# Two kinds of stores issued from Pool's queue, and a new plan of PSUM copies and of the turn to the last stage, in an attention and two feed-forward layers

## The chip, the cores and the metric

One core of a Trainium2 chip runs the whole program. The metric is the device time of one execution in microseconds. Engines are named as in the profile: PE is TensorE's matmul, PEld its weight load, DVE is VectorE, ACT ScalarE, POOL GpSimd, SP SyncE.

## What is computed

A windowed causal attention, then a feed-forward layer with two multiplied branches and two further products, then a second one with a squared ReLU. Everything is fp32.

```python
# attention: B, H, S, D = 4, 8, 576, 64; window 128
scores = np.matmul(q, k.transpose(0, 1, 3, 2)) / np.sqrt(D)
rel = pos[:, None] - pos[None, :]
mask = (rel >= 0) & (rel < window)
scores = np.where(mask, scores - slopes[:, None, None] * np.abs(rel), -1e9)
attn = softmax(scores)            # over the last axis
x = (attn @ v).transpose(0, 2, 1, 3).reshape(B * S, H * D)      # 2304 x 512
# first layer: w1, w2 512 x 1024; w3 1024 x 1024; w_out 1024 x 512
x = (((x @ w1) * (x @ w2)) @ w3) @ w_out
# second layer: w_in 512 x 2048; w_out 2048 x 512
h = np.maximum(x @ w_in, 0.0)
out = (h * h) @ w_out
```

## The kernel before, in words

**Arithmetic.** Outside the attention every fp32 product is made from two fp32r parts of each operand, a high and a low one, in three matmuls (the lines 929 to 931 in the first layer, 1125 to 1127 after it). ScalarE makes the high part by a copy (L196), VectorE or Pool the low one by a subtraction (L199). Blocks of 2 x 2 are multiplied with seven products instead of eight, P1 to P7, so VectorE and Pool also form sums of operands (L716) and of results (L950, L978, L981, L1189, L1236), and ScalarE copies results out of PSUM (tiles d, D, E).

**Stages.** (1) The attention takes 16 pairs of heads. Per pair PE makes the scores (L437) in a first and a second part, VectorE adds the bias and takes the minimum (L405), ScalarE takes the exponent (L413), VectorE the reciprocal of the sums (L422, L423), and `scaled` (L248) normalises on VectorE (L252), ScalarE (L254) or Pool (L250). PE transposes the result (L473), which is copied from PSUM to the tile pt (L196 on ScalarE, L258 on VectorE), multiplies it with v (L497, L513; `p_pv`, `p_pvl`), and `t_xh` copies that product back into the same pt buffer, from which `t_xs` (L526) stores it to x_scr in DRAM. pt has two buffers. While that runs, PE makes the product of w3 with w_out as work of low rank (`p_w34`, L613), which is copied to sg and stored to w_scr by `t_w34` (L621). (2) x is loaded again, split, and multiplied with w1 and w2 (sums d, stored to g_scr). (3) The result times the product of w3 and w_out gives y. (4) y times w_in, with ReLU, goes to s_scr (tiles D). (5) The last stage loads blocks of s_scr (A11, A12, A21, A22; L1297), squares them (L1305), forms sums (L1319), splits them (tiles xA, ww) and multiplies by the second w_out, whose words were merged earlier (`m_scr`) and are loaded back by `m_back`, combined and split (`add_words2`) for each of eight row blocks; "wlao7" is the low part of the last block's word, "wlbo7" that of its sums.

**Order.** Nothing is ordered by hand row by row. The class `Plan` (L31 to L147) is a list scheduler that runs on the host when the program is built: each task has a rank, its engines with a cost, its predecessors, and the buffers it takes and gives back. It keeps a clock per engine; for each task that is ready it picks the engine with the earliest end, to which `bias` (L44) adds a penalty per engine ("d" VectorE, "D" VectorE with a lock shared with "p", Pool; "a" ScalarE), and among the tasks that can start first the one with the lowest rank (`RANK`, L16). If PE would stand still for over 1 us ahead of 40 us of the plan it inserts three small matmuls of an identity, fillers (`p_warm`, L528). The instructions are then written in the plan's order, so each engine and each DMA queue has a fixed order; a latency table (L293) tells the plan how long a result takes to the next engine. "gate" tasks open and close pools: `q1`, `ph`, `q2` (L651 to L669 and L1426 to L1430); q2, the pool of the last stage, takes the place of q1. The list `turn` (L1456) gives the order of the products where the last stage begins. P1 and P2 of the first block are cut in two: Q1 and Q2 accumulate over the row blocks 0 to 5 of the words (18 matmuls each), P1 and P2 over the last two (6 matmuls each); P4 and the others are whole.

All stores and loads are issued by SyncE, one queue, in the plan's order. The tasks of the two stores at issue:

```python
add(f"sx{m}", r + 9, {"dma": w_dma(295)}, lambda e: t_xs(m), [f"xh{g}_{m}" for g in range(2)], [], [f"pt_{m}"])
add(f"sw{fi}", -10, {"dma": w_dma(262)}, lambda e: t_w34(fi), [f"wh{fi}"], [], [f"sg{fi}"])
```

## Time and profile before

| what | value |
|---|---|
| median of 3 runs | 808.65 us (806.52 to 810.44) |
| the profiled execution | 812.59 us, of which the span is 810.8 |
| TensorE busy | 791.7 us of the span |
| VectorE, ScalarE, Pool busy | 612.7, 510.7, 67.9 us |
| mean granted clock of TensorE | 0.989 |
| bytes moved | 155.80 MB, 192 GB/s over the span |

The profile shows one execution. Its span goes from the first to the last instruction; the time of the execution is 1.8 us longer. Busy time counts an engine's instructions; an instruction that issues a DMA is not counted. "A <- B: 2.1, 3, 0.8" in a table of waits means that A's engine stood idle 2.1 us in all, 3 times, 0.8 us at the longest, until B had ended. In a timeline the bracket behind a row gives the idle time ahead of it and what ended it. A granted clock of 1.00 is the full rate.

### The profile page before, as it was taken

What the parts mean: (1) busy time and instruction counts of PE and PEld (TensorE: products, weight loads), DVE (VectorE), ACT (ScalarE), POOL (GpSimd) and SP (SyncE); (2) the same over time, 40 slices, a digit from 0 to 9 for tenths busy, and PEclk for the clock granted to TensorE, in tenths of its full rate; (3) what the DMA queues carried; (4) which work ended last, traced back from release to release, by engine and by line L of the source; (5) the groups of instructions that cost most, each with busy time, mean ns of one, the idle gap of its engine ahead of it and who ended that gap; (6) DMA issues with size and microseconds to landing.
All of it is one profiled execution on the core that took longest, in us unless ns stands there. A gap on an engine that the chain in (4) does not pass through costs nothing. (4 is left out here: it accounts for less than half of the span.)

```text
span 810.8 us, 17310 instructions
## 1 busy us (share of the span) xinstructions
PE 791.7 (98%) x6582; PEld 735.0 (91%) x6582; DVE 612.7 (76%) x1291; ACT 510.7 (63%) x1090; POOL 67.9 (8%) x65
## 2 busy tenths in 40 slices
PE   7989999999999999999999999999998999999998
PEld 6755666689999999899999999999998999999998
DVE  6778687989887787978899955325768997777762
ACT  6988789974554545545655756646766776656630
POOL 1000020111010000200102300001213100000000
PEclk8989999999999999999999999999999999999999
DMA  9987899525887888366754453525654765544200
GB/s 221 289 272 262 250 307 272 179 94 173 308 277 267 279 288 282 123 203 216 219 195 162 160 195 103 201 99 197 203 186 136 193 178 156 142 130 131 79 27 33
DMA packets 115699, 155.80 MB, mean 192 GB/s; under 512 B 12192, under 2 KB 92576, under 8 KB 113568
## 3 DMA queue, kind: packets, MB, share of 16 engines
q1 hardware_dynamic: 115616, 154.70, 61.0%
q8 instruction: 51, 0.84, 0.5%
q14 instruction: 32, 0.26, 0.1%
HBM read 101.71 MB, written 52.95 MB: 191 GB/s over the span
## 5 line engine op out<-in xcount | busy, mean ns | idle before, releaser
L196 ACT ACTIVATE d<-xa 128x288 f32<-128x288 f32 x128 | 52.2, 409 | 97.4 <-PE xa L931 93.3
L1189 DVE TENSOR_TENSOR D<-xb,D 128x384 f32<-128x384 f32 (+1 forms) x62 | 32.1, 520 | 59.3 <-ACT D L196 34.9
L413 ACT ACTIVATE e<-e,st 128x128 f32<-128x128 f32 (+1 forms) x144 | 62.2, 435 | 6.4 <-DVE st L405 5.4
L613 PE MATMUL g<-raw 128*128 128x512 f32 x128 | 63.0, 602 | 0.4 <-DVE raw L335 0.4
L199 DVE TENSOR_TENSOR ww<-fq,ww 128x1024 fp32r<-128x1024 f32 x34 | 41.6, 1223 | 27.0 <-ACT ww L196 26.8
L196 ACT ACTIVATE D<-xa 128x384 f32<-128x384 f32 (+1 forms) x91 | 41.8, 462 | 30.0 <-PE xa L1127 26.4
L196 ACT ACTIVATE ww<-fq 128x1024 fp32r<-128x1024 f32 x35 | 36.9, 1057 | 36.8 <-PE xa L1127 19.9
L931 PE MATMUL xa<-xB,u 128*128 128x288 f32 x192 | 56.8, 296 | 0.0
L929 PE MATMUL xa<-xB,u 128*128 128x288 f32 x192 | 56.8, 296 | 0.0
L930 PE MATMUL xa<-xB,u 128*128 128x288 f32 x192 | 56.1, 292 | 0.0
L1262 ACT ACTIVATE D<-D 128x384 f32<-128x384 f32 x73 | 37.4, 521 | 23.3 <-DVE D L1189 23.3
L716 DVE TENSOR_TENSOR xA<-xA 128x256 f32<-128x256 f32 (+2 forms) x74 | 47.7, 669 | 3.0 <-DMA xA<-g_scr 1.5
L950 DVE TENSOR_TENSOR d<-xb,d 128x288 f32<-128x288 f32 x80 | 36.2, 452 | 15.2 <-ACT d L196 10.8
L473 PEld LDWEIGHTS t<-ident,e 128*128 128x128 f32 x208 | 24.4, 144 | 23.6 <-ACT pt L196 11.2
L405 DVE CUSTOM_DVE_ANT_0 e<-s,bw 128x192 f32<-128x192 f32 (+1 forms) x128 | 40.4, 351 | 2.9 <-PE s L437 2.6
L437 PE MATMUL s<-qk 64*64 64x128 f32 (+2 forms) x768 | 37.5, 293 | 5.0 <-issue 2.1
L437 PEld LDWEIGHTS s<-qk 64*64 64x64 f32 x768 | 28.9, 140 | 13.0 <-issue 4.8
L473 PE MATMUL t<-ident,e 128*128 128x128 f32 x208 | 36.8, 291 | 1.7 <-ACT pt L196 1.3
L930 PEld LDWEIGHTS xa<-xB,u 128*128 128x128 f32 x192 | 36.5, 190 | 0.0
L929 PEld LDWEIGHTS xa<-xB,u 128*128 128x128 f32 x192 | 36.1, 188 | 0.0
L931 PEld LDWEIGHTS xa<-xB,u 128*128 128x128 f32 x192 | 36.0, 188 | 0.0
L1127 PE MATMUL xa<-yA,v 128*128 128x384 f32 x104 | 35.2, 339 | 0.0
(272 smaller groups left out, 2897.9 us busy)
## 6 DMA issues: line engine op xcount, KB each, us to landing
s_scr<-D SPq DMA_DIRECT2D x96, 192.0 KB, 2.0
u<-in_w2io_dram SPq DMA_DIRECT2D x32, 512.0 KB, 6.0
xA<-s_scr SPq DMA_DIRECT2D x20, 512.0 KB, 5.4
qk<-in_qk_dram SPq DMA_DIRECT2D x32, 288.0 KB, 5.4
g_scr<-d SPq DMA_DIRECT2D x64, 144.0 KB, 3.3
xA<-g_scr SPq DMA_DIRECT2D x16, 576.0 KB, 5.5
raw<-in_w3t_dram SPq DMA_DIRECT2D x8, 1024.0 KB, 9.0
raw<-in_w_dram SPq DMA_DIRECT2D x8, 1024.0 KB, 6.9
```

Of the source, the lines that this page charges most:

```text
L196: nc.scalar.activation(out=o, in_=i, func=ACTF.Copy)
L199: eng.tensor_tensor(out=o, in0=a, in1=b, op=ALU.subtract)
L405: nc.vector.tensor_tensor_reduce(out=part_of(m, x, rows), in0=ps, in1=bias, op0=ALU.add, op1=ALU.min, scale=-0.125, scalar=3.0e38, accum_o ...
L413: nc.scalar.activation(out=e, in_=e, func=ACTF.Exp, bias=st[:, 0, x:x + 1], scale=-1.0, accum_out=st[:, 1, x:x + 1],)
L437: nc.tensor.matmul(HD[2 * m + r]["s"][g][o, c:c + w], t[h, 0, 64 * q:64 * q + 64], t[h, 1, 64 * k:64 * k + w], start=True, stop=True,)
L473: nc.tensor.transpose(o, e[:, u:u + 2, :].rearrange("p u c -> p (u c)"), ident)
L613: nc.tensor.matmul(gw[fi], wl, wr, start=c == 0, stop=c == 7)
L716: ENG[e].tensor_tensor(out=o(oi), in0=a(ai), in1=b(bi), op=op)
L929: nc.tensor.matmul(o, wh, xh, start=start and c == 0, stop=False, skip_group_check=True)
L930: nc.tensor.matmul(o, wh, xl, start=False, stop=False, skip_group_check=True)
L931: nc.tensor.matmul(o, wl, xh, start=False, stop=c == len(todo) - 1, skip_group_check=True)
L1262: nc.scalar.activation(out=x, in_=x, func=ACTF.Relu)
```

## The change

It has seven parts. (a) The 16 x stores and the 8 stores of the product are issued from Pool's queue; the plan gets a key "q" for it, with a cost of 1.0 on Pool and a latency of 3.5. (b) The plan's penalties on VectorE fall: d from 1.0 to 0.6, D from 0.2 to 0. (c) The attention's rank h0 goes from -40 to -44. (d) The sums of the last word of the second w_out get a tile of their own, xQ, in the pool q1, in place of xA. (e) The first block's load of A21 waits for the last word, and the split of A12 for its P2 goes to a tile xA in place of u. (f) The gate q2 waits for wlbo7 too. (g) In the list `turn` Q2 stands ahead of P1.

```diff
-RANK = dict(..., c0=0, cj=3, h0=-40, hs=7, ...)
+RANK = dict(..., c0=0, cj=3, h0=-44, hs=7, ...)
...
-    bias = dict(d=1.0, D=0.2, a=0.3, p=0.0)
+    bias = dict(d=0.6, D=0.0, a=0.3, p=0.0)
...
-                    e = q.lower()
+                    e = "p" if q == "q" else q.lower()
...
-            end[n], on[n] = fin, e
+            end[n], on[n] = fin, q if q == "q" else e
...
-                last[h] = max(last[h], fin + (self.lat[e] + 0.5 if e == "dma" else 0.0))
+                last[h] = max(last[h], fin + (self.lat[on[n]] + 0.5 if on[n] in ("dma", "q") else 0.0))
...
-            yA=14, t2a=1, v6=6, D1=2, D2=2, D4=2, D3=1, E1=2, fq=5, ww=4,
+            yA=14, t2a=1, xQ=1, v6=6, D1=2, D2=2, D4=2, D3=1, E1=2, fq=5, ww=4,
...
-        dict(pe=0.25, a=0.3, d=0.22, p=0.25, dma=3.0, gate=0.0),
+        dict(pe=0.25, a=0.3, d=0.22, p=0.25, dma=3.0, gate=0.0, q=3.5),
...
     def t_xs(m):
         b, p = divmod(m, H // 2)
-        nc.sync.dma_start(out=x_scr[b][p], in_=PR[m]["pt"][:, 0:S])
+        nc.gpsimd.dma_start(out=x_scr[b][p], in_=PR[m]["pt"][:, 0:S])
...
-        add(f"sx{m}", r + 9, {"dma": w_dma(295)}, lambda e: t_xs(m), [f"xh{g}_{m}" for g in range(2)], [], [f"pt_{m}"])
+        add(f"sx{m}", r + 9, {"q": 1.0}, lambda e: t_xs(m), [f"xh{g}_{m}" for g in range(2)], [], [f"pt_{m}"])
...
     def t_w34(fi):
-        nc.sync.dma_start(out=w_scr[fi], in_=gw.pop(fi))
+        nc.gpsimd.dma_start(out=w_scr[fi], in_=gw.pop(fi))
...
-        add(f"sw{fi}", -10, {"dma": w_dma(262)}, lambda e: t_w34(fi), [f"wh{fi}"], [], [f"sg{fi}"])
+        add(f"sw{fi}", -10, {"q": 1.0}, lambda e: t_w34(fi), [f"wh{fi}"], [], [f"sg{fi}"])
...
-        pool.update(yA=q, t2a=q, D1=q)
+        pool.update(yA=q, t2a=q, D1=q, xQ=q)
...
-            mw[k, m], sw[k, m] = new(tag, [128, 1024]), new(tag, [128, 768])
+            mw[k, m], sw[k, m] = new(tag, [128, 1024]), new("xQ" if (k, m) == ("o", NM - 1) else tag, [128, 768])
...
-            hold(ss, stag, 6)
+            hold(ss, "xQ" if (k, m) == ("o", NM - 1) else stag, 6)
...
-                + ([] if t == 0 else [f"lf{k}{t - 1}", "wlbo7", ...] if k in ("A11", "A21") else [f"fc1{t - 1}"]), [f"f{k}{t}"])
+                + ([] if t == 0 and k != "A21" else ["wlao7"] if t == 0 else [f"lf{k}{t - 1}", "wlbo7", ...] if k in ("A11", "A21") else [f"fc1{t - 1}"]), [f"f{k}{t}"])
...
-            tag = "u" if (t, P) == (0, 2) else "xA" if P in (1, 2) else "ww"
+            tag = "xA" if P in (1, 2) else "ww"
...
-    add("q2", 0, {"gate": 0.0}, lambda e: open_q2(), last_r + ["wlao5", "wlbo5"] + [...])
+    add("q2", 0, {"gate": 0.0}, lambda e: open_q2(), last_r + ["wlao5", "wlbo5", "wlbo7"] + [...])
...
-    turn = ["Q1o0", "P1o0", "Q2o0", "P2o0", "P4o0", "P6o0", "P7o0", "P5o0"]
+    turn = ["Q1o0", "Q2o0", "P1o0", "P2o0", "P4o0", "P6o0", "P7o0", "P5o0"]
```

What these numbers do to the order of the instructions shows at three places. A row names the line, the operation, the tile written and the tiles read, and its shape.

**SyncE's queue, after the first loads.** qk are q and k of a pair, v its values, raw the weights w3 and w_out, x_scr the attention's result. Before:

```order
L363 DMA qk<-in_qk_dram 64x2x576 x2
L310 DMA raw<-in_w_out_dram 128x2x1024
L315 DMA raw<-in_w3t_dram 128x2048
L526 DMA x_scr_84<-pt 128x576
L363 DMA qk<-in_qk_dram 64x2x576 x2
L368 DMA v_160<-in_v_main_dram 128x2x256
L372 DMA v_160<-in_v_main_dram 64x2x128
L376 DMA v_160<-in_v_main_dram 64x2x64
L377 DMA v_160<-in_v_rest_dram 64x2x64
L310 DMA raw<-in_w_out_dram 128x2x1024
L526 DMA x_scr_84<-pt 128x576
L363 DMA qk<-in_qk_dram 64x2x576 x2
```

And now, from the same load on:

```order
L363 DMA qk<-in_qk_dram 64x2x576 x2
L310 DMA raw<-in_w_out_dram 128x2x1024
L363 DMA qk<-in_qk_dram 64x2x576 x2
L368 DMA v_160<-in_v_main_dram 128x2x256
L372 DMA v_160<-in_v_main_dram 64x2x128
L376 DMA v_160<-in_v_main_dram 64x2x64
L377 DMA v_160<-in_v_rest_dram 64x2x64
L315 DMA raw<-in_w3t_dram 128x2048
L363 DMA qk<-in_qk_dram 64x2x576 x2
L310 DMA raw<-in_w_out_dram 128x2x1024
L368 DMA v_161<-in_v_main_dram 128x2x256
L372 DMA v_161<-in_v_main_dram 64x2x128
```

The x store no longer stands between the loads, and the first load of w_out comes before the fourth pair's q and k. Pool's list holds the stores, in the attention with five of its own operations between them; it runs 53 rows where it ran 46.

**PE in the first two pairs,** from the first transposes (t from e) on; s are scores, a the product with v, the 128x128 matmuls of ident alone the fillers. Before:

```order
L473 MATMUL t<-ident,e 128x128 x4
L437 MATMUL s<-qk 64x192 x2
L437 MATMUL s<-qk 64x128 x2
L437 MATMUL s<-qk 64x64 x2
L437 MATMUL s<-qk 64x192 x2
L473 MATMUL t<-ident,e 128x128 x4
L437 MATMUL s<-qk 64x128 x4
L437 MATMUL s<-qk 64x192 x2
L437 MATMUL s<-qk 64x128 x2
L437 MATMUL s<-qk 64x64 x2
L437 MATMUL s<-qk 64x192 x2
L437 MATMUL s<-qk 64x128 x2
```

And now:

```order
L473 MATMUL t<-ident,e 128x128 x4
L531 MATMUL g<-ident 128x128 x2
L473 MATMUL t<-ident,e 128x128 x4
L437 MATMUL s<-qk 64x192 x2
L437 MATMUL s<-qk 64x128 x2
L437 MATMUL s<-qk 64x64 x2
L437 MATMUL s<-qk 64x192 x2
L473 MATMUL t<-ident,e 128x128
L473 MATMUL t<-ident,e 128x2x64
L473 MATMUL t<-ident,e 128x128 x3
L497 MATMUL a<-pt,v_160 64x192 x2
L497 MATMUL a<-pt,v_160 64x64 x12
```

Before, the second part of the second pair's scores (64x192, 64x128, 64x64, 64x192), the next transposes and the first part of the third pair's stood ahead of the first product with v (L497), which came seven rows behind the first row not shown here. Now that product follows the second part directly, with the pair's last transposes between, and the third pair's first part comes behind it. The whole list has 21 fillers where it had 23.

**ScalarE at the turn** (u, v, ww: high parts; E: a copy of P1's result out of PSUM). Before:

```order
L196 ACTIVATE u<-xA 128x1024
L1262 ACTIVATE D_7506<-D_7506 128x384
L1262 ACTIVATE D_7518<-D_7518 128x384
L196 ACTIVATE ww<-xA 128x1024
L196 ACTIVATE E_7622<-xa 128x256
L196 ACTIVATE ww<-fq 128x1024
L1305 ACTIVATE xA<-xA 128x1024
```

And now:

```order
L1262 ACTIVATE D_7544<-D_7544 128x384
L1262 ACTIVATE D_7519<-D_7519 128x384
L1262 ACTIVATE D_7505<-D_7505 128x384
L1305 ACTIVATE xA<-xA 128x1024
L196 ACTIVATE E_7614<-xa 128x256
L196 ACTIVATE ww<-xA 128x1024
L196 ACTIVATE ww<-fq 128x1024
```

The copy E<-xa stood behind ww<-xA and stands ahead of it now, and u is done earlier. On VectorE the last rows ahead of the sums L1319 were the splits of v and u; now they are two splits of xA, and v, from xQ, is split on Pool.

Counted over the program, VectorE has 111 normalisations of 128x192 where it had 90 (ScalarE none where it had 21); of the copies of D from xa with 128x256, ScalarE has 9 where it had 21 and VectorE 15 where it had 3; up to the first sums L978, VectorE has 12 subtractions xB<-u where it had 2 and 7 sums u<-u where it had 4. Pool has three subtractions xC<-u where it had one and lost those for u.

## Rows read from the trace of the kernel before

**Rows 1.** The page's first part: busy time, share of the span, instructions

```profile
PE 791.7 (98%) x6582; PEld 735.0 (91%) x6582; DVE 612.7 (76%) x1291; ACT 510.7 (63%) x1090; POOL 67.9 (8%) x65
```

**Rows 2.** Windows: length, each engine's busy us, granted clock, DMA share, GB/s

```profile
0.00:20.00 20.00, 15.79 (x171) 13.16 (x172) 12.95 (x67) 12.24 (x44) 3.82 (x18) 0.90 0.94 220
20.00:40.00 20.00, 18.65 (x314) 14.56 (x314) 14.76 (x77) 18.38 (x66) 0.00 (x0) 0.93 0.91 286
40.00:60.00 20.00, 17.00 (x188) 11.67 (x188) 14.99 (x69) 16.97 (x53) 0.00 (x0) 0.83 0.83 283
60.00:160.00 100.00, 99.89 (x1302) 62.58 (x1301) 83.02 (x351) 88.36 (x292) 8.38 (x7) 1.00 0.85 255
180.00:200.00 20.00, 18.46 (x140) 18.23 (x139) 19.86 (x35) 10.35 (x20) 5.09 (x3) 1.00 0.56 176
620.00:640.00 20.00, 17.89 (x129) 17.48 (x128) 18.23 (x21) 13.41 (x18) 1.38 (x1) 0.91 0.78 211
640.00:800.00 160.00, 160.00 (x1336) 160.00 (x1335) 118.44 (x137) 92.52 (x123) 2.73 (x1) 1.00 0.40 112
```

**Rows 3.** PE's waits, 0 to 60 us: total, times, longest

```profile
PE s L437 <- issue: 2.1, 3, 0.8
PE s L437 <- DMA qk<-in_qk_dram: 1.8, 1, 1.8
PE t L473 <- ACT pt L196: 1.3, 3, 0.9
PE s L437 <- DVE st L405: 0.8, 1, 0.8
```

**Rows 4.** SyncE's waits, whole span

```profile
SPq L526 <- ACT pt L196: 42.0, 12, 8.5
```

**Rows 5.** SyncE's timeline: start, us, engine, line, operation

```profile
24.88 0.34 SPq L526 DMA_DIRECT2D x_scr<-pt  x1
```

**Rows 6.** The x store's line L526: who waited for it, and its landings

```profile
  ACT pt L196: 0.6, 1
DMA to landing us min/median/max: 2.1/4.6/7.1
```

**Rows 7.** PE's timeline: first transposes of the third pair

```profile
31.14 0.66 PE L473 MATMUL t<-ident,e 128*128 128x128 f32 x4
```

**Rows 8.** Groups by line and form: busy, mean ns, idle before

```profile
L252 DVE TENSOR_SCALAR e<-e,st 128x192 f32<-128x192 f32 x90 | 23.5, 315 | 0.0
```

**Rows 9.** Timeline of VectorE, Pool and PE, 188 to 194 us

```profile
188.93 1.88 POOL L716 TENSOR_TENSOR u<-u 128x576 f32<-128x576 f32 x1 [7.62 <-DVE u L716]
188.77 0.75 DVE L199 TENSOR_TENSOR xC<-u,xC 128x576 fp32r<-128x576 f32 x1
189.44 2.00 DVE L716 TENSOR_TENSOR u<-u 128x576 f32<-128x576 f32 x1
193.75 0.40 PE L929 MATMUL xb<-xB,u 128*128 128x288 f32 x1 [1.53 <-DVE d L950]
```

**Rows 10.** Timeline of PE, ScalarE and VectorE at the turn

```profile
625.03 0.38 PE L1125 MATMUL xa<-u,xA 128*128 128x256 f32 x1 [0.48 <-ACT u L196]
627.04 0.58 PE L1126 MATMUL xa<-u,xA 128*128 128x256 f32 x1 [1.62 <-DVE u L199]
625.86 1.04 ACT L196 ACTIVATE ww<-xA 128x1024 fp32r<-128x1024 f32 x1
627.87 0.39 ACT L196 ACTIVATE E<-xa 128x256 f32<-128x256 f32 x1 [0.97 <-PE xa L1127]
629.30 1.22 DVE L199 TENSOR_TENSOR ww<-xA,ww 128x1024 fp32r<-128x1024 f32 x1
631.74 0.28 PE L1125 MATMUL xc<-u,ww 128*128 128x256 f32 x1
631.85 0.28 PE L1126 MATMUL xc<-u,ww 128*128 128x256 f32 x1
```

**Rows 11.** Timeline of VectorE ahead of the turn

```profile
618.44 3.49 DVE L199 TENSOR_TENSOR xA<-xA 128x512 fp32r<-128x512 f32 x2
```

More of the change, by code (lines that the diff above doesn't have):

```diff
@@ L13 @@
 ALU = mybir.AluOpType
-RANK = dict(w34=3, vv=20, w0=-15, c0=0, cj=3, h0=-40, hs=7, w12=60, wa=7, wl=9, wb=0, x0=20, mg=4, mgs=1.6, wo=1126, gg=-3, yq=1142)
+RANK = dict(w34=3, vv=20, w0=-15, c0=0, cj=3, h0=-44, hs=7, w12=60, wa=7, wl=9, wb=0, x0=20, mg=4, mgs=1.6, wo=1126, gg=-3, yq=1142)
 B, H, S, D = 4, 8, 576, 64
@@ L111, in run @@
             t, rank, n, q, w = min(near, key=lambda c: (c[1], c[0], c[2]))
-            e = q.lower()
+            e = "p" if q == "q" else q.lower()
             _, _, fn, deps, takes, gives, _ = tasks[n]
@@ L1311, in add_o @@
                 [f"ss{h + 1}{col + 1}r{j}{m}" for m in range(NM)] + ([] if ft[k] == "xA" else ["q2"])
-                + ([] if t == 0 else [f"lf{k}{t - 1}", "wlbo7", *([f"ol1{t - 2}", f"ol7{t - 2}"] if t > 1 else [])] if k in ("A11", "A21") else [f"fc1{t - 1}"]), [f"f{k}{t}"])
+                + ([] if t == 0 and k != "A21" else ["wlao7"] if t == 0 else [f"lf{k}{t - 1}", "wlbo7", *([f"ol1{t - 2}", f"ol7{t - 2}"] if t > 1 else [])] if k in ("A11", "A21") else [f"fc1{t - 1}"]), [f"f{k}{t}"])
         def comb(i, e):
@@ L1429, in fused_kernel @@
     last_r = [f"P{P}r{NJ - 1}{NM - 1}" for P in range(1, 8)]
-    add("q2", 0, {"gate": 0.0}, lambda e: open_q2(), last_r + ["wlao5", "wlbo5"] + [f"ss11r{NJ - 1}{m}" for m in (NM - 2, NM - 1)])
+    add("q2", 0, {"gate": 0.0}, lambda e: open_q2(), last_r + ["wlao5", "wlbo5", "wlbo7"] + [f"ss11r{NJ - 1}{m}" for m in (NM - 2, NM - 1)])
     prev = []
```

## The prediction

> **What bounds the kernel now.** I read the page's first line, then the windows by stage, then PE's waits, and last the stretches where PE stands still. TensorE is busy for 791.7 us of a span of 810.8, VectorE for 612.7, ScalarE for 510.7, Pool for 67.9 [rows 1]. So the kernel is a queue of matrix work, and only the 19 us in which PE does nothing, what its slow clock costs and its filler matmuls can be had back by another order. The windows say where they are [rows 2]: PE works 15.79, 18.65 and 17.00 us in the first three stretches of 20 us, at granted clocks of 0.90, 0.93 and 0.83; from 60 to 160 us it works 99.89 of 100 us at 1.00. Behind that I can tie two places to the change: 180 to 200 us (18.46 of 20), the entry to the stage after the attention, and 620 to 640 us (17.89 of 20, clock 0.91), the turn to the last stage. From 640 to 800 us nothing is idle.
>
> What PE waits for in the first 60 us, behind its start, is mostly four things [rows 3]: 2.1 us for scores whose releaser does not show ("issue"), 1.8 us for one load of q and k, 1.3 us for copies to pt, 0.8 us for a sum on VectorE: 6.0 us. No one engine is late there; PE's written order asks for work a little before it is ready. What is saved there is saved at the end, since from 60 us on PE is full with a fixed list of products.
>
> **The change, part by part.** *The stores of x and of the product go to Pool's queue.* SyncE's queue takes its entries in order, and at the x store it stood 42.0 us in 12 waits for the copies to pt [rows 4]. What stands behind are loads. The first x store goes out at 24.88 us and takes 0.34 [rows 5], and the load of the fourth pair's q and k goes out behind it. The 24 stores take 24 x 0.34 = 8 us off SyncE, for which nobody waits by itself. The loads set free move ahead, but DMA is busy 0.94, 0.91 and 0.83 of the first three stretches [rows 2], so they can come earlier only as far as that leaves room, and PE waited for a load once. So I cost the earlier loads at nothing; what they allow is the new order, below. Against that: a store from Pool has no row in this trace. Its landing is bounded by the stores as they are, 2.1 us at best and 7.1 at worst, median 4.6 [rows 6]. I take the median, since bytes and shape stay. Behind a store stands, through the two pt buffers, the first pt copy of the pair after next. The store of 24.88 lands at about 29.5 by the median; the third pair's first transposes, whose copy fills that buffer, start at 31.14 and take 0.66 [rows 7]: a margin of 2.3 us. Only one copy waited for a store, 0.6 us [rows 6].
>
> The Trainium skill ("DMA: Bandwidth & Descriptors", section "Issuing engines are not separate DMA queues") says that issuing from several engines saves only the time a sequencer takes to issue. By that alone this part would be worth the 8 us of SyncE and nothing at the end. The 42.0 us in SyncE's order are waits and no issue time, so the row goes beyond the rule; on PE's side it has yet to show.
>
> *The attention's order, from the new ranks and biases.* The first part of the third pair's scores now comes behind the first pair's product with v; before it stood ahead and waited 1.8 us for its load. The second part of one pair's scores and the first part of the next pair's no longer follow each other directly; transposes stand between. That joint is the place of the two longest waits called issue, 0.8 us each [rows 3]. Fillers fall from 23 matmuls to 21, worth under 0.5 us. In exchange each product with v follows the last transposes of its pair more closely, and so their copy to pt, where PE waits 1.3 us already. I take half of the 6.0 us as gone, 3.0, since such waits will replace the rest, and 1.5 us for clock and fillers, of 0.17 x 20 = 3.4 us that the 0.83 of one stretch cost and the 0.5. **First stage: -4.5 us.** Best: -(6.0 + 0.5 + 3.4) = -9.9. Worst: new waits for pt, twice today's, +2.6.
>
> *VectorE takes work from ScalarE and Pool.* 21 normalisations of 128x192 go from ScalarE to VectorE, which needs 315 ns for one [rows 8]: +6.6 us. A few copies out of PSUM add some 3 us. Ten more conversions xB<-u and three more sums u<-u of the next stage's operands stand ahead of its first store of a sum, each near the 0.75 us that a like operation takes [rows 9]: 9.8 us. In all about 19 us that VectorE has to do before some 180 us. It works 12.95 + 14.76 + 14.99 + 83.02 = 125.7 of the first 160 us [rows 2], so 34 us are free: the cover holds. Later, 12 copies D<-xa go to VectorE, in the last stage, where PE is full and VectorE busy for 118.44 of 160 us. I cost all this at nothing; if the cover goes, see the third rival.
>
> *The entry to the second stage.* PE waits 1.53 us at 193.75 for a sum d, which is late because a VectorE operation took 2.00 us at 189.44, against 0.75 for one as large just before, while Pool ran a tensor operation of 1.88 us beside it [rows 9], and the next pair alike. So a Pool operation there costs VectorE about 1.2 us. Pool's list at this place changes: fewer u<-u, but three xC<-u where there was one. I take 0, with bounds -1.5 (the wait goes) and +2.4 (two more held up).
>
> *The turn.* Today P1 stands between Q1 and Q2, and PE waits 0.48 us at 625.03 and 1.62 us at 627.04 for ScalarE's and VectorE's halves of the last u [rows 10]. The new order puts Q2 right behind Q1 and P1 after it; the last word's v is split on Pool, from xQ, so that VectorE comes to u sooner. Both waits, 2.1 us, should go. But ScalarE's order now has the copy E<-xa ahead of the conversion ww<-xA for P4, where ww came first. E waits for P1. Q1 ends at 625.03 - 0.48 = 624.55; the 24 matmuls of Q2 and P1, 0.12 us apart at the full clock as in the last two rows, end at 627.4; then E 0.39, ww 1.04 and VectorE's half of ww 1.22 [rows 10] make 630.1, where P4 could start, and not, as now, at 631.74: -1.6. The clock of 0.91 costs 0.09 x 20 = 1.8 us in that stretch [rows 2], and a new wait ahead of P4 may bring the like again. I take **-1.0 us**, with bounds -3.4 (the 1.6 and all of the clock's 1.8) and +2.3: a Pool operation beside VectorE drew out two conversions at 618.44 to 3.49 us [rows 11], where as many elements in one operation take 1.22, and v on Pool may do that once more.
>
> *The rest.* The gate of the last stage waits for the last word now, and the load of A21 too; neither holds up an engine for which PE waits after 640 us, where PE is never idle [rows 2]. The new plan shifts all work between 200 and 600 us a little: 0, with +-1.5, a wait as long as that of 193.75 more or less.
>
> **Sum:** -4.5 + 0 - 1.0 = -5.5 us on the profiled execution's 812.59 us (span 810.8 and 1.8 around it), which gives 807.1. That execution lies 3.9 us above the median of the runs, 808.65; the same step from the median gives **803.2 us**.
>
> **The rivals.** First, *stores from Pool land late*, the case on the slower side. [rows 9, 11] show Pool and VectorE holding each other up for as long as an operation lasts; a store that Pool issues may be held up in the same way. Once a landing exceeds 4.6 + 2.3 = 6.9 us, the first pt copy of each pair from the third on waits, then the next transposes, and PE, whose order is fixed. By the worst landing of now, 7.1, and one hold-up of 1.2 the excess is 8.3 - 6.9 = 1.4 us; over 14 pairs 20 us, and about half, 10, if later pairs have more room. In place of the first stage's gain that gives 808.65 + 10 - 1 = about 818; from 0.4 us of excess a pair on (5.6 us) it eats the whole gain. For it: VectorE gets busier. Against: a quarter of VectorE's time is free, and only one copy ever waited for a store.
>
> The Trainium skill ("SBUF — State Buffer", section "Who interferes with whom") describes this case: a transfer issued from Pool took about 3100 ns instead of 620 beside a VectorE copy. By its 2.5 us more the excess would be 0.2 us a pair, 3 us in all, an estimate from that page, and most of the gain would be gone. No store from Pool is in this trace to test it.
>
> Second, *the waits only move*. DMA at 0.94 and each pair's chain of scores, sums and copies keep setting the pace of the first 60 us; PE waits for the copies as long as it did for scores, and at the turn P4 waits behind E for what Q2 no longer waits. About 808, no change. For it: the waits are of several kinds, none dominant.
>
> Third, *VectorE becomes the bound at the change of stage*. In 180:200 it works 19.86 of 20 us already [rows 2]. If a quarter of the 19 us arrives there, PE waits 5 us more, the first stage's gain is spent, and the time is about 809. Against: the 34 us free before.
>
> **How the numbers follow.** Forecast 0.60; stores late 0.13; waits only move 0.20; VectorE the bound 0.07. A measurement of this kernel tells about 0.5%, 4 us, from no change. So faster 0.60, same 0.20 + 0.05 = 0.25, slower 0.13 + 0.02 = 0.15. The forecast's own bounds go from some 16 us below the median, all best cases together, to no gain. I cut the range at 796, as they hardly come together, and let it reach to 814, which takes in the rivals without a change and the milder half of the first.
>
> **What would show it.** Right: no SyncE waits at x stores; PE busy above 18 us of 20 in 40:60 and a clock above 0.9 there; no wait for u at the turn, a short one for ww ahead of P4, and P4 under 9.8 us behind the start of the turn. Wrong: many waits of a pt copy for the x store, about a microsecond each, and landings above 7 us; a wait for d of over 3 us where the second stage starts; or new waits for pt in the first 60 us as long in sum as those of now.

## The result: 0.5% slower, and the profile after

The changed kernel takes **810.88 us** (median of 18 runs, 808.9 to 818.34), the kernel before 808.36 (18 runs beside them, 806.02 to 810.44). The ratio is 1.0053, 95% interval 1.0038 to 1.0068. The forecast was 803.2: a gain of 5.5 us was foretold and a loss of 2.5 came. The profiled execution after took 810.22 us with a span of 808.5; the one before, with 812.59 and 810.8, stood 4.2 us above its kernel's median, which matters below.

The page's first part and the windows of the changed kernel:

```profile
PE 783.9 (97%) x6578; PEld 726.8 (90%) x6578; DVE 626.9 (78%) x1356; ACT 495.6 (61%) x1043; POOL 60.5 (7%) x73
```

```profile
0.00:20.00 20.00, 16.96 (x234) 14.42 (x235) 12.69 (x71) 13.40 (x52) 3.82 (x18) 1.00 0.92 242
20.00:40.00 20.00, 16.72 (x254) 11.74 (x252) 19.06 (x89) 16.46 (x54) 1.32 (x3) 1.00 1.06 261
40.00:60.00 20.00, 16.07 (x236) 10.51 (x240) 16.23 (x67) 15.20 (x49) 1.78 (x3) 1.00 1.02 295
60.00:160.00 100.00, 95.14 (x1254) 60.91 (x1244) 87.17 (x370) 83.98 (x276) 15.52 (x21) 0.97 0.85 254
...
620.00:640.00 20.00, 19.67 (x148) 19.48 (x147) 18.84 (x25) 17.04 (x24) 2.11 (x1) 1.00 0.84 238
```

Against [rows 2] two things stand out. The turn is mended: PE works 19.67 of 20 us at clock 1.00, where it worked 17.89 at 0.91. But from 60 to 160 us, where it was full (99.89), it now works 95.14, and the first 60 us are no better: 16.96 + 16.72 + 16.07 = 49.75 us against 51.44. Its waits, 0 to 170 us:

```profile
PE t L473 <- ACT pt L196: 8.4, 9, 2.4
PE s L437 <- DVE st L405: 3.3, 1, 3.3
...
PE a L497 <- DMA v<-in_v_main_dram: 0.9, 1, 0.9
PE s L437 <- issue: 0.5, 1, 0.5
```

The waits of [rows 3] for issue and for q and k are nearly gone. In their place PE waits 8.4 us for copies to pt (1.3 before), 7.1 of them in the first 60 us, and once 3.3 us for a sum. What ScalarE and VectorE themselves wait for on DMA there, 0 to 160 us:

```profile
ACT raw L320 <- DMA raw<-in_w3t_dram: 4.3, 2, 3.7
ACT raw L320 <- DMA raw<-in_w_out_dram: 2.8, 3, 1.5
ACT pt L196 <- DMA x_scr<-pt: 2.5, 1, 2.5
ACT raw L320 <- DMA raw<-in_w_dram: 1.6, 1, 1.6
...
DVE raw L329 <- DMA raw<-in_w_dram: 4.7, 2, 3.0
DVE raw L329 <- DMA raw<-in_w_out_dram: 2.2, 1, 2.2
```

That is 15.6 us of waiting for weights that are still on their way (the rows of raw added up), and 2.5 for an x store. Before, the same sum was 1.0 us. Two rows of ScalarE's timeline and one of PE's tie the longest of them to PE's longest wait:

```profile
50.14 1.15 ACT L320 ACTIVATE raw<-raw 128x1024 f32<-128x1024 f32 x1 [3.65 <-DMA raw<-in_w3t_dram]
51.17 0.59 ACT L196 ACTIVATE pt<-t 128x512 f32<-128x512 f32 x1
...
51.81 0.66 PE L473 MATMUL t<-ident,e 128*128 128x128 f32 x4 [2.42 <-ACT pt L196]
```

ScalarE stands 3.65 us at a conversion whose w3 has not landed; the copy to pt is next on its list, and PE's transposes wait for that copy. The 3.3 us for a sum on VectorE go back in the same way to the 3.0 us wait for raw. The x store's line, which is Pool's now, against [rows 4 to 6]:

```profile
L526 POOL DMA_DIRECT2D x_scr<-pt x16: 539/557/842, 20.1 to 164.3; - x16
...
  ACT pt L196: 2.5, 1
...
DMA to landing us min/median/max: 2.4/5.9/8.6
```

SyncE has no such waits left, as foreseen. A store lands after 5.9 us by the median (4.6 before) and 8.6 at worst (7.1), more than the 6.9 that the margin allowed.

SyncE did not become free by it, however. Its waits in the first 160 us add up to 74.8 us where they were 72.8 (in the second executions of both 70.4 and 68.8). It stands at the loads behind the stores now: the loads of q and k (L363) and of v (L368) wait for products of PE to end. The three longest such waits were 2.8, 3.3 and 3.1 us before, and are:

```profile
SPq L363 <- PE s L437: 13.5, 6, 3.3
SPq L368 <- PE a L513: 12.2, 4, 7.4
SPq L363 <- PE t L473: 10.3, 3, 4.2
```

At the end of the attention PE's timeline shows:

```profile
163.05 9.71 PE L613 MATMUL g<-raw 128*128 128x512 f32 x22
172.20 0.70 PE L929 MATMUL xa<-xA,u 128*128 128x288 f32 x1
```

The last product with v has ended, but 22 matmuls of w3 with w_out stand between it and the next stage. Before, that work was spread among the pairs and none was left here. So an attention that ends earlier brings nothing: its gaps were not filled, and the filling is done behind it.

At the turn (timeline of ScalarE and PE, after):

```profile
629.83 0.39 ACT L196 ACTIVATE E<-xa 128x256 f32<-128x256 f32 x1 [0.37 <-PE xa L1127]
630.11 1.06 ACT L196 ACTIVATE ww<-xA 128x1024 fp32r<-128x1024 f32 x1
...
632.45 0.28 PE L1125 MATMUL xc<-u,ww 128*128 128x256 f32 x1
633.17 0.39 PE L1127 MATMUL xc<-u,ww 128*128 128x256 f32 x1 [0.33 <-DVE ww L199]
```

Of the 2.1 us of waits in [rows 10] nothing is left but 0.33. PE's rows from 626.82 on are 24 products into xa (Q1 and P1), then 24 into xc (Q2 and P2), as they were before: the list `turn` allows Q2 ahead of P1, but P1 stayed ahead. What changed is that its operands came in time.

**Where the time went, by stage.** Marks from PE's timelines, in us. Both kernels were profiled twice ("again" are runs e4 and i1).

| mark | before | before again | after | after again |
|---|---|---|---|---|
| end of the last product with v | 167.9 | 163.0 | 163.1 | 158.5 |
| second stage starts (first L929) | 167.8 | 162.9 | 172.2 | 167.5 |
| first L1125 | 438.8 | 435.3 | 445.1 | 440.8 |
| Q1 starts | 621.9 | 617.8 | 626.8 | 622.7 |
| P4 starts | 631.7 | 627.6 | 632.5 | 628.4 |
| end of PE | 807.6 | 799.7 | 805.0 | 802.8 |

The attention with its fillings loses 9.3 us (172.2 - 162.9) or 4.6 (167.5 - 162.9) against the second execution of before, whose granted clock was 1.00 in all of its first 160 us. Some 3 of the 9.3 us are clock: after, it was 0.97 from 60 to 160 us, and 0.50, the lower of its two levels, from 137 to 142 us, right behind the 3.3 us in which PE stood. The second execution of before lies 3.7 us under its kernel's median, so 9.3 is on the high side; by medians the loss apart from the turn is 6.4 us (run e3 below). The turn gives back 4.1 (9.8 us from Q1 to P4 became 5.7); all else is within 2.3.

### The profile page after: what moved, and what is told of

Same layout as the page of the kernel before. It is cut to its first block, busy times and chain, and to the rows that moved or that the text cites. A ratio compares the mean times of both kernels' runs of the same rounds, so it can differ in the third digit from the quotient of the medians.

```text
span 808.5 us, 17313 instructions
## 1 busy us (share of the span) xinstructions
PE 783.9 (97%) x6578; PEld 726.8 (90%) x6578; DVE 626.9 (78%) x1356; ACT 495.6 (61%) x1043; POOL 60.5 (7%) x73
## 3 DMA queue, kind: packets, MB, share of 16 engines
q0 software_dynamic: 1920, 6.82, 2.3%
## 5 line engine op out<-in xcount | busy, mean ns | idle before, releaser
L196 ACT ACTIVATE d<-xa 128x288 f32<-128x288 f32 x124 | 50.5, 408 | 89.6 <-PE xa L931 88.4
L929 PE MATMUL xa<-xB,u 128*128 128x288 f32 x192 | 57.1, 297 | 1.4 <-ACT d L196 0.7
L196 ACT ACTIVATE D<-xa 128x384 f32<-128x384 f32 (+1 forms) x75 | 35.5, 475 | 32.8 <-PE xa L1127 29.1
L929 PEld LDWEIGHTS xa<-xB,u 128*128 128x128 f32 x192 | 36.1, 188 | 2.1 <-ACT d L196 1.2
L252 DVE TENSOR_SCALAR e<-e,st 128x192 f32<-128x192 f32 (+1 forms) x143 | 35.8, 315 | 1.1
```

The source lines that it names most:

```text
L196: nc.scalar.activation(out=o, in_=i, func=ACTF.Copy)
L929: nc.tensor.matmul(o, wh, xh, start=start and c == 0, stop=False, skip_group_check=True)
```

## Experiments

Three theories were put against each other at first: that the stores on Pool's queue cost the time (late landings, pt held longer); that the new order alone costs it, wherever the stores are issued; and that the turn gains while something hides it. Later ones are named where they come up. In the table "before" is the median of the kernel before, run beside it. The ratio is taken from all runs of both and is not the quotient of the two medians, so the two can differ (e1: the medians give 1.0020).

| run | edit | us | before | ratio, 95% |
|---|---|---|---|---|
| e1 | the change's order, stores on SyncE | 809.53 | 807.89 | 1.0038 (1.0007 to 1.0068) |
| e2 | before, only the 24 stores on Pool | 812.32 | 807.89 | 1.0043 (1.0016 to 1.0070) |
| e3 | before and the turn, parts d to g | 804.00 | 807.89 | 0.9938 (0.9912 to 0.9964) |
| e4 | before, one execution | 804.69 | | |
| f1 | the change, stores on SyncE and planned so | 814.35 | 808.24 | 1.0064 (1.0040 to 1.0089) |
| f2 | Pool's stores planned, turn; old biases and rank | 821.86 | 808.24 | 1.0168 (1.0131 to 1.0205) |
| f3 | f1's order, stores on Pool | 814.58 | 808.24 | 1.0079 (1.0051 to 1.0106) |
| f4 | the change, stores booked on the plan's DMA clock | 808.77 | 808.24 | 1.0010 (0.9989 to 1.0031) |
| g1 | e3 and the biases | 818.61 | 806.79 | 1.0135 (1.0096 to 1.0174) |
| g2 | e3 and the rank h0 | 808.42 | 806.79 | 1.0017 (0.9993 to 1.0040) |
| g3 | e2, x stored from a tile of its own | 808.27 | 806.79 | 1.0010 (0.9989 to 1.0032) |
| g4 | f4, x stored from a tile of its own | 800.79 | 806.79 | 0.9915 (0.9882 to 0.9948) |
| h1 | the change, x stored from a tile of its own | 806.08 | 806.88 | 0.9979 (0.9955 to 1.0004) |
| h2 | the change, plan's DMA latency 4.5 for 3.0 | 827.98 | 806.88 | 1.0248 (1.0203 to 1.0293) |
| h3 | g4 with the old biases | 812.30 | 806.88 | 1.0057 (1.0032 to 1.0081) |
| h4 | e3, own tile, stores on SyncE | 807.27 | 806.88 | 0.9997 (0.9972 to 1.0021) |
| i1 | the change again | 811.28 | 807.98 | 1.0018 (0.9986 to 1.0051) |
| i2 | g4 again | 800.87 | 807.98 | 0.9905 (0.9874 to 0.9936) |

**The parts apart: e1 to e4.** e1 keeps every instruction where the change has it and gives the stores to SyncE in that order; e2 is the reverse, the old order with the stores on Pool; e3 has the turn alone (the parts d to g of the change, not shown again); e4 is the kernel before, for a second profile.

```diff
e1, on the change:   -nc.gpsimd.dma_start(out=x_scr...)   +nc.sync.dma_start(out=x_scr...)   (w_scr alike)
e2, on before:       -nc.sync.dma_start(out=x_scr...)     +nc.gpsimd.dma_start(out=x_scr...) (w_scr alike)
```

> The changed kernel's written order of every engine, but the 24 stores issued by SyncE at their place in that order. Theory A (the route over Pool is what costs: landings 5.9 us in place of 4.6 and a pt copy that waits 2.5 us for a store): the landings fall back to about 4.6 us, the 2.4 us gap at 52 us goes, and the time falls by 2.5 us or more from the changed kernel's 810.9, to below 808.5. Theory B (the loads, no longer held back behind the stores, crowd the DMA engines, arrive later than the plan assumes, and conversions of weights stand in VectorE's and ScalarE's order waiting for them): with the stores back in SyncE's order the loads wait again, and come later still for a plan that expects them early; the time stays at 811 or rises by 2 to 8 us. Theory C (the plan's own order of copies and sums): no change, 810 to 812.

> The kernel before, in its own order, with nothing but the issue of the 24 stores moved to Pool's queue. Theory A: later landings, each of some 1.3 us, against a margin of 2.3: between 0 and +6 us. Theory B: SyncE's loads run ahead by as much as 8 us each and crowd the DMA in the first 60 us, but the old order expects them later, so no engine waits for them: between -2 and 0 us. Theory C: no change, within 1 us of 808.4.

> The kernel before with the turn alone changed: own tile xQ, Q2 ahead of P1, the split on xA, the gate and the load of A21. All theories put the loss into the attention, so this should gain what the turn shows in the trace: 2.1 us of waits and up to 1.6 of slow clock, so -2 to -4 us, 804.5 to 806.5. If the turn itself were at fault it would lose.

> The kernel before, unchanged, for a second profile. The first one's execution lay 4 us above the median of its kernel, with a clock of 0.83 from 40 to 60 us and a distance of 120.0 ns between matmuls of 256 columns in the last stage, where the changed kernel has 117.3. If these are marks of that execution, this one shows the attention ending some 3 us earlier than 167.8, and 117.3 ns; if they belong to the kernel, it shows them again.

The turn alone gains 3.9 us (804.0 against 807.89), more than was expected of it. The stores on Pool alone lose 4.4. Taking Pool out of the changed kernel leaves +1.6 of its +2.5. The intervals of e1 and of the change overlap, so no gain is shown, and less moved than either of the first two theories asked for: the order loses without Pool too. The x store of e2 (who waited for it, landings, then ScalarE and PE, and PE's waits for such copies from 0 to 170 us):

```profile
  ACT pt L196: 6.4, 4
...
DMA to landing us min/median/max: 2.4/5.0/9.3
...
76.54 0.60 ACT L196 ACTIVATE pt<-t 128x512 f32<-128x512 f32 x1 [2.83 <-DMA x_scr<-pt]
...
80.99 0.66 PE L473 MATMUL t<-ident,e 128*128 128x128 f32 x4 [1.43 <-ACT pt L196]
...
PE t L473 <- ACT pt L196: 4.5, 8, 1.4
```

Here is the prediction's first rival at work: four copies to pt wait 6.4 us for stores. Behind the longest, at 76.54, ScalarE works without a gap until 80.94, and PE waits 0.43 us for that copy (77.19) and 1.43 for the next (80.99). In all PE waits 4.5 us for such copies, where it was 1.3 and 2.0 in the two executions of before. The rest of e2's loss stands in other waits, 3.7 us for sums (0.8 and 2.0 before) among them; what delays the sums was not followed. e4 corrects the baseline of the prediction. Windows of before, second execution:

```profile
0.00:20.00 20.00, 17.07 (x232) 14.13 (x235) 13.51 (x72) 14.17 (x51) 3.81 (x18) 1.00 0.94 229
20.00:40.00 20.00, 17.13 (x302) 12.94 (x295) 16.84 (x89) 19.24 (x68) 0.00 (x0) 1.00 1.05 322
40.00:60.00 20.00, 17.78 (x189) 10.42 (x180) 17.66 (x76) 19.33 (x64) 0.00 (x0) 1.00 0.90 281
60.00:160.00 100.00, 99.76 (x1290) 62.56 (x1289) 82.54 (x334) 87.48 (x278) 8.16 (x7) 1.00 0.84 250
```

The same program now has the clock at 1.00 in all of the first 60 us, where [rows 2] have 0.90, 0.93 and 0.83, and it ends its attention 4.9 us sooner.

**The plan's numbers: f1 to f4, g1, g2.** The next runs asked whether the new biases and rank, the plan's treatment of Pool's stores, or the stores themselves cost the time. f1 keeps biases, rank and turn but plans and issues the stores on SyncE; f3 has f1's order with the stores issued on Pool; f2 has the stores planned on Pool with the old biases and rank. f4 follows another theory: the plan no longer books the stores' time on its DMA clock, so it thinks that loads land earlier than they do.

```diff
f1, on the change:  -{"q": 1.0}   +{"dma": w_dma(295)}   (w_scr: 262), and nc.sync.dma_start in both
f2, on the change:  -h0=-44 ... bias d=0.6, D=0.0   +h0=-40 ... bias d=1.0, D=0.2
f4, on the change:  +free.update({"dma": max(free["dma"], t) + 0.95} if q == "q" else {})   (behind free[e] = fin)
g1, on e3:          -bias d=1.0, D=0.2   +bias d=0.6, D=0.0
g2, on e3:          -h0=-40   +h0=-44
```

> The whole change but part (a): stores planned and issued on SyncE; new biases, rank h0 and turn stay. Theory D (the plan no longer books the 24 stores, 16 x 0.98 + 8 x 0.87 = 22.7 us, on its DMA line, so it expects loads earlier than they land, conversions of weights wait some 15 us in VectorE's and ScalarE's order, and 11 products are left over behind the attention): all of the loss hangs on (a), so this gives the turn's gain, 802 to 806. Theory A (the route over Pool lands late): the same, 802 to 806. Theory C (biases and rank put too much on VectorE): 809 to 813, with PE waiting for pt copies by 8 us as in the changed kernel.

> The whole change but the biases and the rank: stores planned and issued on Pool's queue, turn changed, biases 1.0 and 0.2, h0 -40. Its plan leaves 11 products over behind the attention, as the changed kernel does. Theory D: as slow as the changed kernel, 808 to 813, with waits of conversions for weights above 10 us. Theory A: what Pool's route cost in the old order, 4.4 us, on top of the turn's 804.0: about 808. Theory C: 803 to 805.

> The order of the run without Pool stores (plan books them on DMA and SyncE), only the issue moved to Pool's queue. Theory A: 4 us above that run, as in the old order (812.3 against 807.9), with pt copies waiting for x stores. Theory D: within 2 us of that run, since the plan books the stores' time; if it lies 4 us above, the route itself costs, whatever the plan.

> The changed kernel, with one line more in the plan: each store on Pool also takes 0.95 us of the plan's DMA line. Stores still go by Pool. Its plan leaves 4 products over where 11 were. Theory D: waits of conversions for weights fall from 15.6 us to below 8, and the time falls by 3 to 7 us, to 804 to 808. Theories A and C: no change, 810 to 812.

> The kernel with the turn alone changed (804.0 us), plus the plan's new biases on VectorE; rank h0 and SyncE's stores as before. Theory C1 (it is the biases that cost the 10 us which biases and rank together cost): 811 to 815, PE waiting for pt copies or for sums. Theory C2 (it is the rank): 803 to 805.

> The kernel with the turn alone changed, plus the rank h0 of -44; biases and stores as before. Theory C1: 803 to 805. Theory C2: 811 to 815. If both this one and the one with the biases lose, any new order of the attention loses against the old one, and the cause is what the plan assumes, not one of its numbers.

All differences here are against the before that ran beside each. Against the turn alone (-3.9 us) the rank costs 5.5 more (g2, +1.6), the biases 15.7 (g1, +11.8), both 10.0 (f1, +6.1), Pool's plan 17.5 (f2, +13.6). All of them together, which is the change, cost 6.4 more (+2.5). So the parts do not add, and no one of them is to blame by itself. f1 tells against both theories that hang the whole loss on the stores: no copy waits for a store in it, its waits for raw are 1.7 us, 2 matmuls are left behind its last pair, and yet it takes 6.1 us more than before, where both had 802 to 806. In its profile (an execution 3.9 us under its median) the second stage starts at 169.6, 164.4 in e3, and takes 276.5 us to the first L1125, 271.5 in e3.

The clock is part of these differences. The mean granted clock of all runs was 0.9918 in f1 and 0.988 in f2, and 0.9964 in before beside them; times some 810 us that is an estimate of 3.7 of f1's 6.1 us and 6.8 of f2's 13.6. In e3 it was 0.9987 against 0.9962, 2.0 of the 3.9 gained.

f2 lies far above what any theory gave it; its timelines show the same chain as e2's, longer (ScalarE, then PE):

```profile
61.58 0.60 ACT L196 ACTIVATE pt<-t 128x512 f32<-128x512 f32 x1 [4.18 <-DMA x_scr<-pt]
...
62.23 1.12 PE L473 MATMUL t<-ident,e 128*128 128x128 f32 x4 [5.37 <-ACT pt L196]
```

f3 does not differ from f1, although two copies in it wait 4.1 us for stores: there they were not what PE waited for last. g1 loses most of its time not in the attention but in the second stage (283 us from the first L929 to the first L1125, 271.5 in e3). ScalarE and PE there:

```profile
340.22 0.68 ACT L196 ACTIVATE xB<-xA 128x576 fp32r<-128x576 f32 x1 [4.11 <-DMA xA<-g_scr]
340.81 0.39 ACT L196 ACTIVATE d<-xa 128x288 f32<-128x288 f32 x1
...
341.25 0.40 PE L929 MATMUL xa<-xB,u 128*128 128x288 f32 x1 [3.24 <-ACT d L196]
```

This is the picture of 50.14 us again, with another load: a conversion stands on ScalarE until its operand has been loaded, and the copy that PE needs is behind it. f4 (+0.5) is 2.0 us better than the change. Its interval ends at 1.0031, under that of the change (from 1.0038), but meets that of the change run again (i1 below), so this gain is likely and not shown. Its waits for raw fell to 5.1 us, as foreseen, while its time stayed above the 804 to 808 that were expected; its copies to pt wait 7.0 us for stores.

**The stores' source: g3, g4, h1, h4.** Theory: a store from pt holds one of the two pt buffers until it has landed. If t_xh copies to a tile of its own (one buffer, px), the copies to pt no longer wait for stores. Two small tiles of sums share one allocation to make room, which no run does by itself.

```diff
-            copy(e, PR[m]["pt"][:, q:q + w], PR[m][g][:, c:c + w])
+            copy(e, PR[m]["px"][:, q:q + w], PR[m][g][:, c:c + w])
...
-        nc.gpsimd.dma_start(out=x_scr[b][p], in_=PR[m]["pt"][:, 0:S])
+        nc.gpsimd.dma_start(out=x_scr[b][p], in_=PR[m]["px"])
```

> The old order with the 24 stores issued by Pool, as in the run that took 812.3 us, but the attention's result is copied into a tile of its own, so a pt buffer no longer waits for a store (the two small tiles of sums share one allocation to make room). Theory A (the pt copies' waits for stores, 6.4 us in 4, are what Pool's route costs): 807 to 809.5, and no wait of a pt copy for a store. Theory B (the loads set free crowd the DMA, or Pool and VectorE hold each other up): still 811 to 813.

> The change with the stores' time booked on the plan's DMA line (808.8 us), and the attention's result in a tile of its own as well. Theory A: its pt copies waited 7.0 us in 3 for stores, with PE gaps of 2.9 and 1.8 us; these go and the time falls by 3 to 5 us, to 804 to 806, about the turn alone. Theory B: 808 to 809.

> The changed kernel, its order kept, with the attention's result in a tile of its own, so that no pt buffer waits for a store. Theory A (waits of pt copies for stores): in this kernel's trace one such wait, 2.5 us, with a PE gap of 2.4 us: the time falls by 2 to 4 us, to 807 to 809. The rest of the loss in its attention, waits of conversions for weights (15.6 us on ScalarE and VectorE), stays. If it falls to 804 or below, the stores were the whole loss; if it stays above 810, they were not in it.

> The turn alone (804.0 us) with the attention's result in a tile of its own, stores on SyncE. There the pt copies wait 0.4 us for stores, so Theory A: no change, 803 to 805. If it takes 801, the own tile and not Pool's queue is what makes the version of 800.8 us fast.

In the old order the loss by Pool falls from 4.4 us (e2) to 1.5 (g3), and what is left has one wait, for the only px:

```profile
ACT px L196 <- DMA x_scr<-px: 2.7, 1, 2.7
```

In the changed kernel the tile turns +2.5 us into -0.8 (h1, each against the before that ran beside it), and no copy to pt waits for a store any longer; PE waits 3.9 us for such copies where it was 8.4. h1's interval lies wholly under that of the change (the wider one of the change run again, i1, it still meets), and the rows of e2 and f2 show the wait at work, so the buffer's hold is taken as shown for the changed kernel. In the old order the intervals of e2 and g3 still overlap, and it is likely. With SyncE's stores, which land sooner, the tile costs time: h4 has e3's order, one px wait of 3.0 us, and stands at +0.4 us where e3's -3.9 was expected to hold, and the intervals of the two do not meet. Why it costs as much as that is open. With the stores' time booked as well, g4 takes 800.79, better than expected and better than h1: their intervals do not meet. So the unbooked time is a cause too, at 5.2 us beside the own tile (-6.0 against -0.8). That it works through the waits for weights alone is not shown: they are 6.2 us in h1's profile and 15.6 and 6.3 in the two of the change, and in g4's (ScalarE and VectorE, 0 to 160 us):

```profile
ACT raw L320 <- DMA raw<-in_w_out_dram: 4.0, 2, 2.5
...
DVE raw L329 <- DMA raw<-in_w3t_dram: 0.2, 1, 0.2
```

Behind its last pair 8 matmuls of w3 with w_out are left, 22 in the change, and its second stage starts at 162.5 (164.7 when run again), about as early as that of before in its better execution.

**Two controls: h2, h3.** h2 asks whether a plan that merely takes every load to be later does what the booking does; h3 takes back the biases in the fastest version.

```diff
h2, on the change:  -dma=3.0   +dma=4.5
h3, on g4:          -bias d=0.6, D=0.0   +bias d=1.0, D=0.2
```

> The changed kernel with one number of the plan changed: a DMA's latency 4.5 in place of 3.0, so that conversions are put later against their loads. Theory D (the plan expects loads before they land): the waits of conversions for weights fall from 15.6 us to below 8 and the time by 2 to 5 us, to 806 to 809. Against it: 811 or more, with the waits gone and the time the same.

> The version of 800.8 us (stores booked on the plan's DMA line, own tile), with VectorE's old biases of 1.0 and 0.2. In the kernel with SyncE's stores the new biases cost 14 us. If biases cost by themselves: 793 to 798. If it is the match of plan and chip, and not VectorE's load: 799 to 806, either sign.

h2 went the other way: 828 us, though its waits for raw fell to 4.3 us. Its losses are spread over all stages (PE's waits add up to 30.6 us in all, 20.5 in the change), so this theory holds only in part: late weights are one way to lose, and a plan that avoids them by delaying everything loses more elsewhere. In h3 the old biases cost 11.4 us, where in e3's plan the new ones had cost 15.7. The same numbers are good in one plan and bad in another.

**The change and the fastest version again: i1, i2.** The programs of the change and of g4, unaltered, to see what one profile is worth.

> The changed kernel, unchanged, for a second trace. If what its first trace shows belongs to the kernel and not to that execution: the products' stage starts between 170 and 174 us, 11 products stand behind the last pair, one pt copy or more waits for a store by 2 us or more, conversions wait for weights above 10 us in sum, and the time is 809 to 813.

> The version with the stores' time booked and the own tile once more, beside the changed kernel on the same chip. It took 800.8 us: 799 to 803 again, 8 to 11 us below the changed kernel, and 4 to 8 below the kernel before.

The change took 811.28 us again, 3.3 above before by the medians, though this interval takes in no change at all. Its profiled execution has fewer of the waits than the first and than was expected: 6.3 us for raw in place of 15.6, one wait of 0.5 for a store in place of 2.5. The waits for copies to pt stay (5.7 us in 7), 22 matmuls stand behind the last pair again, and the second stage starts at 167.5, still 4.6 late. So the size of each wait belongs to the execution, the kind of chain to the order. **The fastest version held**: 800.87, ratio 0.9905, 7.1 us below before and 10.4 below the change, both run beside it.

## Why the prediction was wrong, point by point

*The stores.* Right: SyncE's 42 us of waits at the stores went, and PE's wait for q and k, 1.8 us, fell to 0 and 0.6 in the two executions of the change. Wrong: "I take the median, since bytes and shape stay". The landing from Pool was 5.9 and 5.3 us in the two executions of the change, 5.0 in the old order, and up to 9.7 at worst, against a margin of 2.3 us over 4.6. That is the rival *stores land late*, which had a chance of 0.13: its mechanism is shown (h1, with the rows of e2 and f2), at 4.4 us alone and 3.3 inside the change, under half of the 10 it was priced at, because one to four copies wait and not 14. The Trainium skill ("SBUF — State Buffer", section "A bandwidth-pool intuition that's wrong (but worth ruling out)") gives a slowing from about 620 to about 3100 ns for such a transfer beside a VectorE copy. Here, in one and the same order, Pool for SyncE moved the median by 0.4 us (e2 against before), 1.5 (f3 against f1) and nothing (the change against e1), and the worst by 2.2, 1.9 and 0.6: in this kernel the effect is far smaller. Part of the late landing is the order's: e1's stores, from SyncE, took 5.9 us too.

The sentence "I cost the earlier loads at nothing" failed as well. The loads of weights were to be earlier; what came was an order that asked for them earlier still. In the two executions of the change ScalarE and VectorE stood at their conversions for 15.6 and 6.3 us, where it had been 1.0 and 0.8. And the loads did not run free: SyncE's waits moved from the stores to the loads (74.8 us against 72.8). One reason for the late weights is that the plan lost the stores' time from its DMA clock: with that time booked they fell to 5.1 us in f4. Booking it was worth 5.2 us (g4 against h1), 2.0 without the own tile (f4). The Trainium skill ("DMA: Bandwidth & Descriptors", section "Issuing engines are not separate DMA queues") had it that another issuing engine saves issue time alone; by the time of the kernel the trace agrees, though the waits on SyncE were 42 us: e2 took the stores off SyncE and gained nothing.

*The attention's order, -4.5 us.* **This is the step that failed.** It became a loss: 4.6 and 9.3 us in the profiles, 6.4 by the medians (the change against e3). Of its terms, 3.0 were for waits that were to go, and "such waits will replace the rest" was too mild: those for pt went from 1.3 to 8.4 and 5.7 us, beyond the bound of "twice today's". The 1.5 for clock and fillers was no property of the old order at all: e4 shows it at clock 1.00, and the change lost some 3 us by a clock of 0.97 from 60 to 160 us. And the reckoning ended at 60 us. The first four pairs did become faster (the fourth product with v ends at 46.5 and 49.3 us, 50.4 in e4), but PE's filling work slid behind the last pair, 22 matmuls in 9.7 us; the windows from 60 to 160 us, which I took to be full for good, lost 4.6 us.

*VectorE takes work, at nothing.* The cover in busy time was there (VectorE 78% in all), and the third rival did not come: VectorE is not the bound at the change of stage. But a share of busy time does not say what stands behind what. The biases that move this work cost 15.7 us in e3's plan (g1) and saved 11.4 in g4's (h3 taken against it). By which waits they do that in each plan I have not settled; g1's 4.11 us stall is one.

*The entry to the second stage, 0.* Right in sum: from the first L929 to the first L1125 it takes 272.9 and 273.3 us, 271.0 and 272.4 before.

*The turn, -1.0.* The sign was right, the size not: by the medians it is -3.9, past the bound of -3.4, which the interval of e3 (-7.1 to -2.9) takes in. I had P4 behind the 24 matmuls of Q2 and P1 and then E and ww, 8.2 us behind Q1's start. The row of the plan was misread: P1 stays ahead of Q2, so E and ww are made beside Q2 and P2, and P4 follows 5.7 us behind Q1. The slow clock went too: from 620 to 640 us it is 0.91 in both executions of before and 1.00 in both of the change.

*The baseline.* "The same step from the median" moved the sum from the profiled 812.59 to 808.65, but kept terms (1.5 us of clock) that belonged to that one execution.

## What to carry to other kernels

In a statically ordered kernel, price a new order by what stands behind each waiting instruction on its engine, to the end of the stage and not of the stretch that looked idle; an engine with a quarter of its time free can still be the one that everybody waits for. If a transfer moves to another queue, keep its time in the scheduler's transfer clock, and do not let it hold a buffer that the next step of the pipeline needs: these two repairs turned a loss of 2.5 us into a gain of 6 to 7. Profile the kernel before twice before a term is drawn from its clock or from one wait, and take the parts of a change one by one only as a hint, since they need not add.

## What the hardware showed beyond that

In the last stage PE is never idle in either kernel, and yet two executions of the same program differ there by 3.8 us (175.9 and 172.1 us from P4 to the end, before and before again). Windows of the two, in that order:

```profile
640.00:790.00 150.00, 150.00 (x1252) 150.00 (x1251) 114.29 (x131) 90.40 (x121) 2.73 (x1) 1.00 0.42 118
```

```profile
640.00:790.00 150.00, 150.00 (x1280) 149.99 (x1279) 113.27 (x131) 88.13 (x117) 2.03 (x1) 1.00 0.41 116
```

The granted clock is 1.00 in both, but 1252 matmuls stand in the first and 1280 in the second: 119.8 and 117.2 ns for one (150 us over the count). What sets this the trace does not show. The stretches with a granted clock under 1.00 also fall elsewhere in each execution of one program. An x store takes Pool 0.56 us to issue by the median (SyncE: 0.33), and lands at best after 2.4 us (2.1). The 24 stores also got a DMA queue of their own, where all loads and stores had gone through one. The page of the changed kernel (packets, MB, share):

```profile
q1 hardware_dynamic: 112160, 147.88, 59.7%
q0 software_dynamic: 1920, 6.82, 2.3%
```

The one queue of before took 115616 packets, 3456 more, so the same bytes of the stores went in 1920 packets in place of 3456. The forecast, which took the landing from SyncE's stores, did not know of this.
